# Gated attention and two feed-forward layers on one core: the state's product in quadrants, a first chunk without gap transfers, other fillers, and the last stores from two queues

## The chip, the cores and the metric

The kernel runs on one core of one Trainium2 chip. The metric is the device time of a run in microseconds; lower is better. The profile is of one execution, and its times count from the start of its span.

## The reference

For each of 4 batches and 8 heads a recurrence runs over 768 steps with a state of 48 x 48; its output is reordered to 3072 tokens of 384 features and goes through two feed-forward layers:

```python
for t in range(S):                     # q, k, v, alpha: (4, 8, 768, 48), float32
    state = alpha[:, :, t, :, None] * state + np.einsum('bhd,bhe->bhde', k[:, :, t], v[:, :, t])
    y[:, :, t] = np.einsum('bhd,bhde->bhe', q[:, :, t], state)
...
h = x @ w_in                           # 3072 x 384 by 384 x 2048
g = np.where(h > 0.0, h, np.exp(np.minimum(h, 0.0)) - 1.0)
x = g @ w_out                          # 2048 x 384
...
g = x @ w_gate                         # 384 x 1536
silu = g * (1.0 / (1.0 + np.exp(-g)))
out = silu * (x @ w_val) @ w_out       # 1536 x 384
```

## The kernel before

**Units.** The sequence is cut into 6 chunks of 128 steps. A chunk of one batch is a unit, 24 in all; a unit holds the 8 heads as 4 pairs, head j of a pair in partitions 64j to 64j+47 (`PR` = 112 partitions with the hole between them). A unit's input, 1 MB, has four parts: gate F, K, Q and V. VectorE scans F (`A`), VectorE, ScalarE and, from unit 4 on, GpSimd scale K and Q by the running product of the gates or its inverse (`N`, `M`). Then TensorE takes four steps: `Dk` transposes K (`flip`; ScalarE's `keep` copies it to KT), `E` makes the scores K'Q of each head (`scores`; VectorE's `causal` masks them into A), `Gs` makes the outer product of KT and V that renews the state (`outer`; VectorE's `state` adds and scales it into `sc[b]`), and `Hy` makes the output (`values`). For chunks after the first, `values` multiplies the state with Q by one 112 x 112 matmul a pair, with a block-diagonal copy `sbd` of the state that ScalarE makes in two instructions; it then adds V times A, one matmul for each head, 64 and 48 columns wide. All float32 matmuls show as two instructions each.

**Layout of x.** The result of a unit has 4 pairs of 2 x 48 rows, but the first layer wants 3 tiles of 128 rows. Pairs 0 to 2 go to rows 0 to 47 and 64 to 111 of the three tiles (`high`, and `low` or, in the first chunk, `minus` and `rest`, make the two float32r parts). The fourth pair goes to a tile `x3`, and when the four units of a chunk are there, `gaps` moves it by six DMAs in pieces of 16 rows into the holes. The rows of `w_in` are permuted to fit (`_feature_order`).

**Layers.** The first layer (`moe1`) makes, for each block f of 128 hidden features and 512 tokens, 9 matmuls of 512 columns into `h` and 9 into `acc`; between them ScalarE and VectorE compute elu and split it in two parts. It runs in the order of `SEGMENTS`: both of the first two chunks with the first half of the features, then both with the second half, then whole chunks. Units of a later chunk are mixed in. Weights come as int64 views of 768 KB (`weight`), and ScalarE and VectorE turn each into two float32r parts, three instructions each; two raw buffers (`RAWS`) take turns. The second layer (`moe2`) makes 18 matmuls into `gv` and 12 into `q` for each of 12 blocks in each of 6 chunks; for the last block of a chunk each of the four `q` tiles is copied out, in turn by ScalarE and VectorE, and stored by SP.

**Order.** Every step is put into a plan (`Plan.add`) with its engine, an assumed duration, and what it reads and writes. `Plan.run` schedules the list by assumed times and then issues it in the order of the planned starts, and `Pinned` keeps this order on each engine. `fill` is called before each planned TensorE step up to the first product of the first layer, with the planned gap in front of it; `warm` then issues bf16 matmuls on zeros (`idle` in the profile) for this gap, one for each 0.22 us:

```python
if ops[i][0] == "PE" and fill and start[i] <= start[until]:
    fill(start[i] - last)
    last = start[i] + ops[i][1]
...
for _ in range(int((us - 0.2) / 0.22)):
    ten.matmul(out=self.idle, lhsT=self.z, rhs=self.z[:, None, :].to_broadcast([128, 4, 128]), ...)
```

Before the plan, `at.warm(6.8)` (L821) issues such matmuls too. PSUM has two places that units share with nobody in the later chunks: `aps` (one bank: transpose, outer product, values) and `ape` (two banks: scores).

Of the kernel before, what the change touches and what calls it, by code (L numbers as in the profile page):

```python
# [18 lines left out]
DM = H * D  # L19
# [5 lines left out]
KD = DM // 128  # L25
TB = B * C
NF1, NF2 = F1 // 128, F2 // 128
G = 2
# [7 lines left out]
MINUS = B  # L36
# [5 lines left out]
class Plan:  # L42
# [25 lines left out]
    def run(self, fill=None, until=0):  # L68
# [72 lines left out]
def kernel(  # L141
# [52 lines left out]
    def weight(plan, pool, tag, src, slots):  # L194
# [5 lines left out]
        def load():  # L200
            w.raw = P.rp.tile([128, WT, 2], I32, tag="raw", name="raw")
            syn.dma_start(out=w.raw.rearrange("p a t -> p (a t)"), in_=src.bitcast(I32))
# [35 lines left out]
        plan.add("SP", 0.5, load, w=[hk, lk], kb=768)  # L238
# [22 lines left out]
    class Attention:  # L261
        def __init__(self, es):
# [7 lines left out]
            self.sbd = [cp.tile([128, NP, 128], F32, name=f"sbd{b}") for b in range(2)]  # L270
# [5 lines left out]
            self.neg = cp.tile([128, 128], F32R, name="neg")  # L276
            self.x3 = cp.tile([128, 2, TB], F32R, name="x3")
# [20 lines left out]
        def init(self):  # L298
            vec.memset(self.zero, 0.0)
# [4 lines left out]
            make_identity(nc, self.ident)  # L304
            vec.tensor_scalar(
# [8 lines left out]
            for t in self.sbd:  # L314
                nc.gpsimd.memset(t, 0.0)

        def warm(self, us):

            if self.idle is None:
                self.z = self.cp.tile([128, 128], BF16, name="wz")  # L320
                vec.memset(self.z, 0.0)
                self.idle = ph.tile([128, TB], F32, tag="h", name="idle")
            for _ in range(int((us - 0.2) / 0.22)):
# [94 lines left out]
        def Dk(self, u):  # L418
# [16 lines left out]
            plan.add("PE", 0.45, flip, r=[K], w=[key], soon=SOON, lag=MARGIN)  # L435
            plan.add("ACT", 0.48, keep, r=[key], w=["KT"])

        def E(self, u):
            d, (F, K, Q, V) = self.u[u], self.keys(u)
            c, b = divmod(u, B)  # L440
            if c:
                def state():
                    for j in range(2):
                        r = slice(64 * j, 64 * j + D)
                        act.activation(
                            out=self.sbd[u % 2][r, :, 64 * j:64 * j + D], in_=self.sc[b][r], func=AF.Copy)
                plan.add("ACT", 0.65, state, r=[("sc", b)], w=[("sbd", u % 2)])
# [25 lines left out]
            plan.add("PE", 1.25, scores, r=[K, Q], w=keys, soon=SOON, lag=MARGIN)  # L473
            plan.add("DVE", 1.24 if len(keys) > 1 else 1.1, causal, r=keys, w=["A"])

        def Gs(self, u):
# [27 lines left out]

            plan.add("PE", 0.75, outer, r=["KT", V], w=[key], soon=SOON, lag=MARGIN)
            plan.add("DVE", 0.65 if c else 0.3, state, r=[key, F], w=[("sc", b)])

        def Hy(self, u):
            d, (F, K, Q, V) = self.u[u], self.keys(u)
            c, b = divmod(u, B)  # L510
            key, bank = self.bank(u)
            ts = slice(b * C, (b + 1) * C)
            xk, gk = ("x", c % 2, b), ("x3", b)

            def values():
                v = d["v"]
                d["oy"] = o = bank()
# [7 lines left out]
                for p, cs in enumerate(cols):  # L525
                    ten.matmul(
                        out=o[0:64, cs], lhsT=v[:, 2 * p, :], rhs=d["A"][:, 0, p],
                        start=not c and p == 0, stop=p == NP - 1,
                    )
                    ten.matmul(  # L530
                        out=o[64:PR, cs], lhsT=v[:, 2 * p + 1, 0:D], rhs=d["A"][:, 1, p],
                        start=not c and p == 0, stop=p == NP - 1,
                    )
# [530 lines left out]
```

## Time and profile before

| what | value |
|---|---|
| median of 3 runs | 989.59 us (989.09 to 989.59) |
| the profiled execution's own time | 990.69 us |
| its span, first to last instruction | 988.9 us |
| TensorE busy | 98% of the span |
| VectorE, ScalarE, GpSimd busy | 55%, 52%, 7% |
| mean granted TensorE clock | 0.999 |
| share of `gv`, `q`, `h`, `acc` in the chain that ended last | 30%, 15%, 18%, 19% |

A busy time is the union of the instructions of an engine, fillers included; matmuls overlap, so that a busy TensorE can still be doing less than it could. The windows of the profile show the same by stage. In a timeline, instructions of one kind in a row are merged, with their count; what stands in brackets is how long the engine had been idle and what released it. PE is TensorE, DVE VectorE, ACT ScalarE, POOL GpSimd; SPq are the DMA issues of SP.

### The profile page before, as it was taken

Reading aid. Unit: us, or ns where it says so; the run is one execution under the profiler, and the core shown is the slowest. Engines: PE = TensorE matmul, PEld = TensorE weight load, DVE = VectorE, ACT = ScalarE, POOL = GpSimd, SP = SyncE. Lnnn points to the kernel's source line nnn. Section 1 sums busy time; section 2 is a strip of 40 time slices with the busy share of each in tenths; the row PEclk is TensorE's granted clock in tenths of the full one; section 3 lists DMA queues with packets and bytes.
Section 4 is the critical chain, followed back from the end, with each engine's and each line's share of the span. In section 5 each row is a group of like instructions: output and inputs, shape, how many; then the busy total and the mean of one; then the engine's idle time right before and its main releaser. Section 6 shows DMA issues by size and latency. Waiting matters only on the chain.

```text
span 988.9 us, 13352 instructions
## 1 busy us (share of the span) xinstructions
PE 973.4 (98%) x5354; PEld 811.2 (82%) x5354; DVE 541.0 (55%) x840; ACT 512.7 (52%) x910; POOL 69.3 (7%) x51
## 2 busy tenths in 40 slices
PE   9899999999999999999999999999999999999997
PEld 4577788878887888888888888888888888888886
DVE  4999888667646653533677763334333334333332
ACT  3889999666776765555898542212212212212111
POOL 0122011123211310100000000000000000000000
PEclk9999999999999999999999999999999999999999
DMA  4646434333302301100434311001001001000001
GB/s 192 222 158 209 162 114 159 108 102 118 101 1 85 129 6 43 36 14 1 160 128 183 127 52 65 1 1 64 1 1 57 8 1 45 9 1 32 1 1 36
DMA packets 20662, 72.51 MB, mean 73 GB/s; under 512 B 2672, under 2 KB 5744, under 8 KB 17648
## 3 DMA queue, kind: packets, MB, share of 16 engines
q1 hardware_dynamic: 20592, 71.58, 21.2%
q8 instruction: 44, 0.72, 0.3%
q14 instruction: 26, 0.21, 0.1%
HBM read 58.20 MB, written 11.01 MB: 70 GB/s over the span
## 4 chain that ended last, share of the span: by engine, by line
PE 91%; ACT 3%; DVE 3%; DMA 2%; issue 0%; SPq 0%; ACTq 0%; DVEq 0%
PE gv L128 30%; PE acc L128 19%; PE h L128 18%; PE q L128 15%; PE aps L128 4%; PE idle L128 2%; PE ape L128 2%; DMA in<-qkva 1%; DVE in L128 1%; ACT raw L128 1%; DVE raw L128 1%; DMA raw<-w 1%; ACT e L128 1%; ACT R L128 1%; ACT x L128 0%
## 5 line engine op out<-in xcount | busy, mean ns | idle before, releaser
L128 PE MATMUL gv<-x,wt 128*128 128x512 f32 x1296 | 308.1, 391 | 0.0
L128 PEld LDWEIGHTS gv<-x,wt 128*128 128x128 f32 x1296 | 242.2, 188 | 48.0
L128 PE MATMUL h<-x,wt 128*128 128x512 f32 x864 | 215.6, 394 | 1.4 <-DMA x<-x 1.4
L128 DVE TENSOR_TENSOR s<-gv,s 128x512 f32<-128x512 f32 x144 | 99.6, 691 | 210.7 <-ACT s L128 167.3
L128 PE MATMUL acc<-g,wt 128*128 128x512 f32 x864 | 214.5, 393 | 0.2 <-DVE g L128 0.2
L128 PEld LDWEIGHTS h<-x,wt 128*128 128x128 f32 x864 | 159.7, 188 | 37.0 <-ACT r L128 1.7
L128 PEld LDWEIGHTS acc<-g,wt 128*128 128x128 f32 x864 | 160.4, 188 | 35.0 <-DVE g L128 0.6
L128 PE MATMUL q<-wt,u 128*128 128x384 f32 x864 | 163.0, 337 | 0.0
L128 PEld LDWEIGHTS q<-wt,u 128*128 128x128 f32 x864 | 153.6, 188 | 5.6
L128 ACT ACTIVATE s<-gv 128x512 f32<-128x512 f32 x72 | 43.1, 598 | 176.6 <-PE gv L128 176.6
L128 DVE SCALAR_TENSOR_TENSOR e<-e,r 128x512 f32<-128x512 f32 x96 | 68.6, 715 | 98.0 <-ACT r L128 97.9
L128 ACT ACTIVATE u<-s 128x512 fp32r<-128x512 f32 x72 | 45.4, 631 | 123.6 <-DVE s L128 123.2
L128 ACT ACTIVATE e<-h 128x512 f32<-128x512 f32 x96 | 57.1, 595 | 67.8 <-PE h L128 67.4
L128 DVE TENSOR_TENSOR g<-e,g 128x512 fp32r<-128x512 f32 x96 | 67.3, 701 | 29.8 <-ACT g L128 29.5
L128 ACT ACTIVATE g<-e 128x512 fp32r<-128x512 f32 x96 | 60.3, 628 | 28.9 <-DVE e L128 28.5
L128 DVE SCALAR_TENSOR_TENSOR raw<-raw 128x768 int32<-128x768 int32 x68 | 67.9, 1000 | 12.0 <-ACT raw L128 10.9
L128 DVE TENSOR_TENSOR u<-s,u 128x512 fp32r<-128x512 f32 x72 | 49.8, 692 | 40.6 <-ACT u L128 40.5
L128 ACT ACTIVATE e<-e 128x512 f32<-128x512 f32 x96 | 60.7, 632 | 2.9
L128 ACT ACTIVATE raw<-raw 128x768 f32<-128x768 f32 x68 | 58.9, 905 | 3.1 <-DMA raw<-w 2.9
L128 ACT ACTIVATE r<-h 128x512 f32<-128x512 f32 x96 | 55.9, 582 | 0.0
L128 POOL TENSOR_TENSOR in<-in 112x512 f32<-112x512 f32 x20 | 30.1, 1504 | 249.9 <-DVE in L128 130.7
L128 POOL TENSOR_TENSOR in<-in,R 112x512 f32<-112x512 f32 x20 | 37.0, 1849 | 79.5 <-ACT R L128 79.5
(78 smaller groups left out, 614.7 us busy)
## 6 DMA issues: line engine op xcount, KB each, us to landing
raw<-w SPq DMA_DIRECT2D x34, 768.0 KB, 4.2
in<-qkva SPq DMA_DIRECT2D x23, 1024.0 KB, 5.4
x2r<-x2d SPq DMA_DIRECT2D x18, 256.0 KB, 3.4
out<-y SPq DMA_DIRECT2D x24, 192.0 KB, 2.0
x2d<-o SPq DMA_DIRECT2D x12, 256.0 KB, 2.3
x<-x SPq DMA_DIRECT2D x36, 64.0 KB, 4.3
half<-o SPq DMA_DIRECT2D x6, 256.0 KB, 4.0
part<-half SPq DMA_DIRECT2D x6, 256.0 KB, 6.1
```

Source lines behind the costliest of these rows:

```text
L128: ins = getattr(self.engine, name)(*a, **k)
```

## The change

Seven things change together.

1. **State's product.** `sbd` and its copies go. `values` multiplies `sc[b]` itself, 48 x 48 for each head, 8 matmuls instead of 4. Pairs 2 and 3 are written crosswise: head i of pair p goes to output half j = i xor `CROSS[p]`. V's product stands first, then the state's product in the order of pairs 0, 2, 1, 3, so that four matmuls in a row read and write the four quadrants. The output lies over the inner halves of the two banks of `ape`, no longer in `aps`.
2. **Joined steps.** From unit 4 on, scores and transpose of a unit are one step of the plan, and outer product and values another.
3. **First chunk.** `Hy` calls a new function `first`: it multiplies A of the fourth pair with V's 16-column pieces padded by zeros (`vz`, copied by GpSimd), so that the rows of the holes come out in their place. The first chunk has no `x3` and no `gaps`; one ScalarE instruction makes each part.
4. **Weights.** Because pairs are crossed, the third tile of `w_in` has its halves of 64 rows exchanged: each `w_in` load is three DMAs.
5. **Fillers.** `at.warm(6.8)` goes. The first gap gets one filler for each 0.36 us, later gaps one for each 0.25 us.
6. **Last chunk.** ScalarE issues the stores of tiles 0 and 2. The last tile is copied in halves by ScalarE and VectorE, and stored in halves by ScalarE and SP.
7. `gaps` of the later chunks reads the crossed rows.

```diff
@@ Plan.run @@
-                fill(start[i] - last)
+                fill(start[i] - last, last)
@@ weight @@
+            to, of, n = w.raw.rearrange("p a t -> p (a t)"), src.bitcast(I32), 2 * G * 128
+            if not cross:
+                syn.dma_start(out=to, in_=of)
+                return
+            m = n * CROSS.index(1)
+            syn.dma_start(out=to[:, 0:m], in_=of[:, 0:m])
+            for j in range(2):
+                syn.dma_start(
+                    out=to[64 * j:64 * j + 64, m:KD * n], in_=of[64 - 64 * j:128 - 64 * j, m:KD * n])
...
-        plan.add("SP", 0.5, load, w=[hk, lk], kb=768)
+        plan.add("SP", 1.5 if cross else 0.5, load, w=[hk, lk], kb=768)
@@ init, warm @@
+            self.z = self.cp.tile([128, 128], BF16, name="wz")
+            vec.memset(self.z, 0.0)
...
+            nc.gpsimd.memset(self.vz, 0.0)
...
-            for t in self.sbd:
-                nc.gpsimd.memset(t, 0.0)
...
-            for _ in range(int((us - 0.2) / 0.22)):
+            for _ in range(int((us - 0.2) / (0.25 if start else 0.36))):
@@ Dk, E @@
-            if c:
-                def state():
-                    for j in range(2):
-                        r = slice(64 * j, 64 * j + D)
-                        act.activation(
-                            out=self.sbd[u % 2][r, :, 64 * j:64 * j + D], in_=self.sc[b][r], func=AF.Copy)
-                plan.add("ACT", 0.65, state, r=[("sc", b)], w=[("sbd", u % 2)])
...
+                def both():
+                    scores()
+                    flip()
+                plan.add("PE", 1.65, both, r=[K, Q], w=[*keys, key], soon=SOON, lag=MARGIN)
+                plan.add("ACT", 0.48, keep, r=[key], w=["KT"])
@@ first @@
+            def apart():
+                pool.tensor_copy(
+                    self.vz[:, :, :, D:64],
+                    d["v"][:, 2 * KD:H, 0:D].rearrange("p j (i e) -> p j i e", i=KD))
+
+            def values():
+                d["oy"] = o = bank()
+                for p in range(KD):
+                    for j in range(2):
+                        i = j ^ CROSS[p]
+                        ten.matmul(
+                            out=o[64 * j:64 * j + 64, p * C:(p + 1) * C], lhsT=d["v"][:, 2 * p + i, :],
+                            rhs=d["A"][:, i, p], start=p == 0, stop=False)
+                for p in range(KD):
+                    for j in range(2):
+                        i = j ^ CROSS[p]
+                        ten.matmul(
+                            out=o[64 * j:64 * j + 64, p * C:(p + 1) * C], lhsT=self.vz[:, i, p],
+                            rhs=d["A"][:, i, KD], start=False, stop=p == KD - 1)
...
+            def high():
+                if 0 not in xt:
+                    new_x(0)
+                act.activation(
+                    out=xt[0][:, 0, :, ts], in_=d["oy"][:, 0:KD * C].rearrange("p (a c) -> p a c", a=KD),
+                    func=AF.Copy)
...
+            def minus():
+                ten.matmul(
+                    out=d["oy"][:, 0:KD * C], lhsT=self.neg, rhs=xt[0][:, 0, :, ts],
+                    start=False, stop=True, skip_group_check=True)
...
+            plan.add("POOL", 0.4, apart, r=[V], w=["vz"], port=True)
+            plan.add("PE", 1.5, values, r=["A", V, "vz"], w=[key], soon=SOON, lag=MARGIN)
+            plan.add("ACT", 0.45, high, r=[key], w=[xk])
+            plan.add("PE", 0.25, minus, r=[xk], w=[key], soon=SOON)
+            plan.add("ACT", 0.45, rest, r=[key], w=[xk])
@@ Hy, from unit 4 on @@
+                o = self.pe.tile([128, 2, 512], F32, tag="ape", name="ape").rearrange("p a n -> p (a n)")
+                d["oy"] = o = o[:, 256:768]
                 cols = [slice(p * C, (p + 1) * C) for p in range(NP)]
                 for p, cs in enumerate(cols):
-                    if c:
+                    for j in range(2):
+                        i = j ^ CROSS[p]
                         ten.matmul(
-                            out=o[0:PR, cs], lhsT=self.sbd[u % 2][0:PR, p, 0:PR], rhs=d["Q"][0:PR, p],
-                            start=p == 0, stop=False,
+                            out=o[64 * j:64 * j + (D if j else 64), cs],
+                            lhsT=v[:, 2 * p + i, 0:D] if j else v[:, 2 * p + i, :],
+                            rhs=d["A"][:, i, p], start=p % 2 == 0, stop=False,
                         )
...
+                for p in range(2):
+                    for pp in (p, p + 2):
+                        for i in range(2):
+                            j = i ^ CROSS[pp]
+                            r = slice(64 * i, 64 * i + D)
+                            ten.matmul(
+                                out=o[64 * j:64 * j + D, cols[pp]], lhsT=self.sc[b][r, pp],
+                                rhs=d["Q"][r, pp], start=False, stop=p == 1,
+                            )
...
+                def both():
+                    outer()
+                    values()
+                plan.add("PE", 2.2, both, r=["A", V, Q, "KT", ("sc", b)], w=[key, okey],
+                         soon=SOON, lag=MARGIN)
+                plan.add("DVE", 0.65, state, r=[okey, F], w=[("sc", b)])
@@ gaps, step @@
+                        k = 64 * (j ^ CROSS[i] ^ CROSS[KD]) + GAP * i
...
-            if b == B - 1:
+            if b == B - 1 and c:
                 self.gaps(c)
...
-            if nxt:
+            if nxt and u + 1 < B:
                 self.Dk(u + 1)
@@ moe2, last chunk @@
+                        def left(t=t, o=o, es=hs[0]):
+                            place()
+                            half(o.t[:, es], accs[t][:, es], 0)
+                            store(act, o, t, es)
...
+                        plan.add("ACT", 0.4, left, r=[("q", t)], w=[o.key])
+                        plan.add("DVE", 0.3, right, r=[("q", t)], w=["right"])
+                        plan.add("SP", 0.5, lambda t=t, o=o, es=hs[1]: store(syn, o, t, es), r=["right"])
...
+                        if end and t % 2 == 0:
+                            plan.add("ACT", 0.1, lambda t=t, o=o: store(act, o, t), r=[o.key])
@@ the start @@
-    at.warm(6.8)
     at.init()
```

## Rows read from the trace of the kernel before

**Rows 1.** page, part 1: busy us (share of the span) xinstructions
```profile
PE 973.4 (98%) x5354; PEld 811.2 (82%) x5354; DVE 541.0 (55%) x840; ACT 512.7 (52%) x910; POOL 69.3 (7%) x51
```

**Rows 2.** windows: length, busy us of each engine (instructions), clock, DMA share, GB/s
```profile
20.76:48.30 27.54, 23.57 (x245) 14.72 (x245) 26.98 (x49) 23.30 (x49) 2.59 (x2) 1.00 0.51 182
48.30:54.00 5.70, 4.82 (x49) 2.88 (x46) 4.55 (x10) 4.80 (x9) 1.86 (x1) 1.00 0.81 226
54.00:100.00 46.00, 44.73 (x332) 36.05 (x330) 45.57 (x70) 42.04 (x79) 12.30 (x8) 1.00 0.53 182
100.00:150.00 50.00, 49.67 (x269) 40.82 (x270) 42.62 (x59) 46.52 (x80) 4.64 (x3) 1.00 0.40 136
```

**Rows 3.** timeline, 0 to 30 us: start, length, engine, what [idle before]
```profile
1.07 18.50 PE L128 MATMUL idle<-wz 128*128 128x512 bf16 x72 [1.07 <-DVE zero L128]
...
9.85 0.69 DVE L128 SCALAR_TENSOR_TENSOR in<-N,in 112x512 f32<-112x512 f32 x1 [0.19 <-ACT N L128]
...
12.28 0.68 DVE L128 TENSOR_TENSOR in<-in 112x512 f32<-112x512 f32 x1
...
19.50 1.16 PE L128 MATMUL acc<-in 48*128 48x128 f32 x16
...
20.76 1.29 DVE L128 TENSOR_TENSOR A<-acc,mask 128x512 int32<-128x512 int32 x2 [7.80 <-PE acc L128]
```

**Rows 4.** timeline of TensorE, windows 2 to 6 and 8 to 12 us
```profile
1.47 4.90 PE L128 MATMUL idle<-wz 128*128 128x512 bf16 x11
...
7.75 4.48 PE L128 MATMUL idle<-wz 128*128 128x512 bf16 x20
```

**Rows 5.** timeline, 45 to 55 us
```profile
47.69 0.64 ACT L128 ACTIVATE x<-acc 112x128 fp32r<-112x128 f32 x2
...
48.36 3.94 SPq L128 DMA_DIRECT2D x<-x  x6
...
54.01 1.19 PE L128 MATMUL h<-x,wt 128*128 128x512 f32 x4
```

**Rows 6.** timeline of TensorE, one unit from 296 us
```profile
299.28 0.67 PE L128 MATMUL aps<-in,KT 128*64 128x48 f32 x16
299.88 2.33 PE L128 MATMUL h<-x,wt 128*128 128x512 f32 x9
302.05 1.04 PE L128 MATMUL aps<-in,sbd 112*112 112x128 f32 x8
303.02 1.09 PE L128 MATMUL aps<-A,in 128*64 128x128 f32 x16
304.03 2.35 PE L128 MATMUL acc<-g,wt 128*128 128x512 f32 x9
306.32 1.16 PE L128 MATMUL ape<-in 48*128 48x128 f32 x16
307.41 0.60 PE L128 MATMUL aps<-ident,in 112*128 112x112 f32 x4
307.78 2.29 PE L128 MATMUL h<-x,wt 128*128 128x512 f32 x9
```

**Rows 7.** timeline of TensorE, 30 to 60 us: a unit of the first chunk
```profile
36.09 0.67 PE L128 MATMUL acc<-in,KT 128*64 128x48 f32 x16
36.59 1.37 PE L128 MATMUL aps<-A,in 128*64 128x128 f32 x16
```

**Rows 8.** timeline of TensorE, 100 to 116 us: blocks with no unit between
```profile
102.52 2.20 PE L128 MATMUL acc<-g,wt 128*128 128x512 f32 x9
104.56 2.20 PE L128 MATMUL h<-x,wt 128*128 128x512 f32 x9
```

**Rows 9.** DMA issues at 2.5 to 2.8 us: count, KB each, us to landing
```profile
raw<-w SPq DMA_DIRECT2D x1, 768.0 KB, 12.0
```

**Rows 10.** timeline, 980 to 989 us
```profile
980.93 2.95 SPq L128 DMA_DIRECT2D out<-y  x4
...
981.98 0.56 DVE L128 COPY y<-q 128x384 f32<-128x384 f32 x1 [0.48 <-PE q L128]
```

More of the change, by code (lines that the diff above doesn't have):

```diff
@@ L25 @@
 KD = DM // 128
+CROSS = (0, 0, 1, 1)
 TB = B * C
@@ L191, in __init__, with weight @@
             self.key = key
-    def weight(plan, pool, tag, src, slots):
+    def weight(plan, pool, tag, src, slots, cross=False):
         w = Box(*turn(tag, slots))
@@ L433, in keep @@
                     out=d["KT"].rearrange("p a c -> p (a c)"), in_=d["ok"][:, 0:NP * PR], func=AF.Copy)
-            plan.add("PE", 0.45, flip, r=[K], w=[key], soon=SOON, lag=MARGIN)
-            plan.add("ACT", 0.48, keep, r=[key], w=["KT"])
+            if u < B:
+                plan.add("PE", 0.45, flip, r=[K], w=[key], soon=SOON, lag=MARGIN)
+                plan.add("ACT", 0.48, keep, r=[key], w=["KT"])
+            return key, flip, keep
         def E(self, u):
@@ L471, in causal @@
                     )
-            plan.add("PE", 1.25, scores, r=[K, Q], w=keys, soon=SOON, lag=MARGIN)
+            turned = self.Dk(u) if u >= B else None
+            if turned:
+                key, flip, keep = turned
+                def both():
+                    scores()
+                    flip()
+                plan.add("PE", 1.65, both, r=[K, Q], w=[*keys, key], soon=SOON, lag=MARGIN)
+                plan.add("ACT", 0.48, keep, r=[key], w=["KT"])
+            else:
+                plan.add("PE", 1.25, scores, r=[K, Q], w=keys, soon=SOON, lag=MARGIN)
             plan.add("DVE", 1.24 if len(keys) > 1 else 1.1, causal, r=keys, w=["A"])
@@ L503, in state, with first, rest @@
                 vec.tensor_tensor(out=sc[0:PR], in0=kv, in1=pc, op=ALU.mult)
+            if c:
+                return key, outer, state
             plan.add("PE", 0.75, outer, r=["KT", V], w=[key], soon=SOON, lag=MARGIN)
-            plan.add("DVE", 0.65 if c else 0.3, state, r=[key, F], w=[("sc", b)])
+            plan.add("DVE", 0.3, state, r=[key, F], w=[("sc", b)])
+        def first(self, u):
+            d, (F, K, Q, V) = self.u[u], self.keys(u)
+            key, bank = self.bank(u)
+            ts = slice(u * C, (u + 1) * C)
+            xk = ("x", 0, u)
+            def apart():
[26 more added lines that the diff above has]
+                    start=False, stop=True, skip_group_check=True)
+            def rest():
+                act.activation(
+                    out=xt[0][:, 1, :, ts], in_=d["oy"][:, 0:KD * C].rearrange("p (a c) -> p a c", a=KD),
+                    func=AF.Copy)
+            plan.add("POOL", 0.4, apart, r=[V], w=["vz"], port=True)
[3 more added lines that the diff above has]
+            plan.add("ACT", 0.45, rest, r=[key], w=[xk])
@@ L737, in load_split, with moe2 @@
         return b
-    def moe2(plan, x, xs, w2, pools, yp, put):
+    def moe2(plan, x, xs, w2, pools, yp, put, end=False):
         accs, us = {}, {}
@@ L804, in prep_w1 @@
         g, s = divmod(i, 2)
-        w1[g, s] = weight(plan, lambda: P.wp, "w", w1d[g, s], 2 * NG1)
+        w1[g, s] = weight(plan, lambda: P.wp, "w", w1d[g, s], 2 * NG1, not (plan.now or s))
     def prep_w2(plan, i, pool, n):
```

79 lines of the change are left out of this document (36 added, 43 removed).

## Prediction, on record before the result

> **What bounds the kernel now.** I read the page first, then the stages, then the timeline of the stage in which no engine ought to be waiting. The page says that TensorE is busy for 973.4 us of a 988.9 us span [rows 1], so time can come only from work that TensorE does and from TensorE work that is filler. The stages [rows 2] split the run. From 100 us on TensorE is full (49.67 of 50 us) and VectorE has slack (42.62). Between 20.76 and 100 us it is VectorE that is full: 26.98 of 27.54, then 4.55 of 5.70, then 45.57 of 46.00. All that it idles there is 0.56 + 1.15 + 0.43 = 2.1 us. The timeline of the first 25 us [rows 3] then shows what the page hides: 72 filler matmuls hold TensorE from 1.07 to 19.57 us. K of unit 0 is finished by VectorE at 9.85 + 0.69 = 10.54, VectorE runs out of other work at 12.28 + 0.68 = 12.96, and it then waits 7.80 us for the scores, which come behind the fillers at 19.50. So there are three regimes: a start bound by filler, a stretch to 100 us bound by VectorE, and the rest by TensorE.
>
> **Start.** The old call asks for int((6.8 - 0.2)/0.22) = 30 fillers before the plan; the other 42 of the 72 mean that the plan puts its first TensorE step at 42 to 43 times 0.22 plus 0.2, or 9.44 to 9.66 us. The 30 go, and the same gap divided by 0.36 gives 25 or 26. The fillers' spacing shows two levels [rows 4]: 11 in 4.90 us (0.45 each), later 20 in 4.48 us (0.22 each), that is, a clock of half and of full speed. The faster level was there by 7.75 us; from there to 19.57 about 53 fit, so some 19 were issued before. Of 26 fillers the last 7 take 7 x 0.22 = 1.5 us, and TensorE is free near 9.4 us, 1.1 us ahead of K. The scores (1.16 us) end before 12.96, so VectorE goes on without the wait: 20.76 - 12.96 = **7.8 us**. Nothing new is late there: the first weight piece lands 2.67 + 12.0 = 14.7 us after the start [rows 9], 1.7 us after VectorE goes on. From below, 6.5 us if that landing holds ScalarE up for most of this; from above, 19.50 - 10.54 = 9.0 us, TensorE's own wait.
>
> **First chunk without the transfer of gaps.** The first x is now whole when ScalarE has written it. Before, ScalarE ends at 47.69 + 0.64 = 48.33, six DMAs are issued for 3.94 us, and the first product starts at 54.01 [rows 5]. TensorE may thus start 5.7 us earlier relative to the others. But behind it VectorE is full to 100 us, and everything that it does there is due by then (elu, eight weight pieces, four units). TensorE would only wait in smaller portions. What can be won is VectorE's idle time of 2.1 us; I take half, **1.0 us** (0 to 5.7). The added cost lies on engines with cover: four more products of 128 columns a unit, in TensorE time that is filler anyway; one small GpSimd copy; and ScalarE writes one 384-column tile where it wrote two. If VectorE's queue were not the bound there, those products would cost about 4 x 4 x 0.12 = 2 us.
>
> **Weights in three transfers.** Eight loads become 24 issues on SP. At 3.94/6 = 0.66 us an issue [rows 5] each such load lands up to 1.3 us later, and unit loads queue behind it. Half of the eight fall into the VectorE stretch; two raw buffers cover most. I take **-0.5 us** (0 to -2.5).
>
> **A unit's TensorE work.** In the TensorE-bound part each microsecond of a unit counts, for 16 units (chunks 2 to 5); those of chunk 1 lie in VectorE's stretch. Step prices by start-to-start in one unit [rows 6]: the transposed K's outer product 0.60, the state's product 0.97 (8 instructions, 0.121 each), the product with V 1.01, scores 1.09 (16 instructions, 0.068 each: two of them run at once), transpose 0.37. A block of nine big matmuls takes 2.04 between others [rows 8], but 304.03 to 306.32 = 2.29 between two steps of split tiles, and 299.88 to 302.05 = 2.17 behind one. So entering or leaving a split costs 0.12 to 0.13.
> - Joining the outer product and V's product saves one leaving, 0.13. Where they already stand together the outer product takes 36.59 - 36.09 = 0.50, not 0.60 [rows 7]. Together 0.23.
> - The state's product: 8 instructions of 112 x 112 become 16 of 48 x 48. The trace has no four at a time. If four run at once, that is 4 steps of 0.121 = 0.48 instead of 0.97. If two, 8 steps: 0.97. If one, 16 steps: 1.94. The nearest rows are the scores (two row halves at once) and V's product (two column halves at once); nothing in them excludes both together, and the pairs are issued so that the two writers of one output half go to different banks. I take four, and 0.07 for the added change of form: saving 0.42.
> - In chunk 5 there is no outer product; V's product now needs an entry of 0.12 which the state's full-size product did not: saving 0.30.
> - Joining scores and transpose gives little, since they often stand together already (as at 307.41), and a small step that stands beside another today saves an entry and a leaving, 0.25, which the new order may lose. The new neighbours are unknown; I take off 0.1 a unit, 1.6 us.
>
> Sum: 12 x 0.65 + 4 x 0.30 - 1.6 = **7.4 us**; with two at once 16 x 0.49 = 7.8 us less, so -0.4; with one at once 16 x 1.46 = 23.4 us less, so -16. The ScalarE copies of the state (one of 0.7 us a unit) go too; from 100 us ScalarE is off the path, so this is worth nothing by itself.
>
> **End.** The last copy runs 981.98 to 982.54; the fourth store's issue ends at 980.93 + 2.95 = 983.88, 1.34 us behind it, because three issues stand ahead on SP [rows 10]. Halves shorten the copy by about 0.2 us (an estimate: less than half of 0.56, as a fixed part stays). An issue takes 2.95/4 = 0.74 us on average. SP's half then ends its issue near 981.98 + 0.36 + 0.74 = 983.1, 0.8 earlier; but ScalarE must issue the third tile's store before it copies its half, and issue again, which comes to 981.98 + 0.74 + 0.36 + 0.74 = 983.8, 0.1 earlier. I take half-way, **0.5 us** (-0.5 to 1.0).
>
> **Sum.** 7.8 + 1.0 - 0.5 + 7.4 + 0.5 = 16.2 us. The profiled execution took 990.69 us (span 988.9), so 974.5; the median of the runs is 1.1 lower, 989.59 - 16.2 = **973.4 us**.
>
> **Rivals.**
> - *The quadrants run two at a time.* The 16 small products need 8 steps, and the units' gain is gone: 973.4 + 7.8 = 981.2. For it: both halves of one pair write one PSUM bank, where the scores' halves today write different ones. Against it: V's two halves write one bank at once today, in disjoint output partitions. The Trainium skill (TensorEngine Tiling (Array Packing), Gotcha 1: PSUM Pressure) says that different row tiles cannot access the same PSUM bank simultaneously; taken literally for whole banks, it gives this rival's time. No row of this trace shows the case.
> - *The quadrants run one by one, and the kernel gets slower.* 16 steps a unit: 973.4 + 23.4 = 996.8, slower by 7.2. It decides from 16.2/16 = 1.0 us more for a unit's state product than I give it, that is above about 1.5 us. Against it: every split form in the trace overlaps at least in pairs.
> - *The early product counts in full.* If the plan can put off VectorE work beyond 100 us, where VectorE has 7.4 us of slack in 50, TensorE's 5.7 us come out whole: 973.4 - 4.7 = 968.7. Against it: all eight weight pieces were needed by then.
> - *The front gives back less.* Another wait takes the filler's place: the weight landing, SP's longer queue, or a TensorE clock at its lower level because fewer fillers bridge the gaps. Half of the start's 7.8 and nothing of the 1.0 would be left, 5 us less: 978.4. For it: the landing at 14.7 is close. Against it: VectorE waits for nothing else in 7.80 us.
>
> **How the numbers follow.** The forecast has 0.55, pairs 0.17, less at the front 0.13, the early product in full 0.10, one by one 0.05. The range runs from just below the third rival (967) to just above the first (982). A change of 0.2%, 2 us, is what a measurement of this kernel can tell from none. Only the one-by-one case is slower, 0.05; gains that add up to under 2 us, 0.01; the rest is faster, 0.94.
>
> **What would show it.** Filler: 25 or 26 of them ahead of the first scores, these near 10.6 us, and no VectorE wait of more than 1 us before the mask step. Start of the TensorE-bound part near 92 us, where it was 100.33. Small products in the 48 x 48 form, 16 in about 0.5 us; 0.97 or more means pairs. No DMA from x to x before the first big product, which starts near 40 us, with TensorE waits between 40 and 90 us of some 5 us in all. The last store's issue end about 1 us behind the last copy. The prediction falls if the quadrants don't overlap, or if VectorE is not the bound that I read between 20 and 100 us.

## The result, and the profile after

The changed kernel takes 981.7 us, median of 8 runs (977.56 to 984.53); the kernel before took 989.62 beside it (988.22 to 991.75). The ratio is 0.9917, with a 95% interval of 0.9898 to 0.9936. The gain is 7.9 us where 16.2 were forecast; the time lies inside the range, at its upper edge. The profiled execution took 980.24 us with a span of 978.8 us.

The page's busy times and its granted clock in 40 slices:

```profile
PE 955.5 (98%) x5471; PEld 797.8 (82%) x5471; DVE 544.7 (56%) x840; ACT 498.6 (51%) x863; POOL 74.1 (8%) x54
PEclk8989999999999999999999999999999999999999
```

TensorE's busy time, fillers included, fell by 17.9 us and the span only by 10.1 [rows 1], so waits came in, and the clock line says where to look: slices 1 and 3, the first 75 us. The same stages as in [rows 2], cut where the changed kernel has them: first mask, first big product, first big product of chunk 1, and 50 us more (length, then busy us of PE, PEld, DVE, ACT and POOL, granted clock, DMA share, GB/s):

```profile
14.45:43.21 28.76, 23.80 (x253) 16.31 (x251) 26.39 (x45) 20.63 (x35) 4.51 (x6) 0.86 0.44 149
43.21:99.22 56.01, 48.44 (x400) 37.71 (x400) 51.19 (x82) 44.42 (x80) 18.30 (x9) 0.94 0.59 187
99.22:149.22 50.00, 50.00 (x271) 41.03 (x272) 42.69 (x58) 46.49 (x79) 7.00 (x4) 1.00 0.45 152
```

VectorE, which idled 2.1 us between 20.76 and 100 us before, now idles 28.76 + 56.01 - 26.39 - 51.19 = 7.2 us ahead of chunk 1. The clock is below full in both stages, where it was full before. Two stretches hold most of that, and a third comes ahead of them, around the first scores:

```profile
11.70:19.00 7.30, 7.30 (x58) 5.12 (x60) 7.04 (x15) 5.72 (x10) 0.00 (x0) 0.53 0.50 159
...
39.00:43.00 4.00, 3.44 (x42) 2.85 (x38) 4.00 (x8) 2.11 (x4) 1.22 (x2) 0.57 0.00 0
...
56.00:63.90 7.90, 7.34 (x47) 5.82 (x49) 6.96 (x9) 6.24 (x11) 0.78 (x1) 0.57 0.37 133
```

The start of TensorE's timeline, beside [rows 3]:

```profile
1.07 8.53 PE L128 MATMUL idle<-wz 128*128 128x512 bf16 x29 [1.07 <-DVE zero L128]
11.69 0.57 PE L128 MATMUL aps<-ident,in 112*128 112x112 f32 x4 [2.08 <-DVE in L128]
12.24 2.08 PE L128 MATMUL acc<-in 48*128 48x128 f32 x16
```

The fillers end at 9.60, and then TensorE idles for 2.08 us, because VectorE finishes K of unit 0 at 10.89 + 0.69 = 11.58 where it was 10.54 before. A scan of the next unit now stands ahead of it:

```profile
7.57 1.37 DVE L128 TENSOR_TENSOR_SCAN in<-in,zero 112x128 f32<-112x128 f32 x4 [0.65 <-DMA in<-qkva]
...
10.89 0.69 DVE L128 SCALAR_TENSOR_TENSOR in<-N,in 112x512 f32<-112x512 f32 x1
```

When TensorE goes on, its clock falls to the lower level (0.50, 1.2 of 2.4 GHz), and the scores take 2.08 us where they took 1.16. The first mask still starts at 14.45 instead of 20.76.

TensorE's waits over the whole span (us in total, times, longest):

```profile
PE h L128 <- DMA x<-x: 3.4, 1, 3.4
PE acc L128 <- ACT KT L128: 3.3, 2, 2.6
PE ape L128 <- DVE x L128: 2.7, 1, 2.7
PE aps L128 <- DVE in L128: 2.1, 1, 2.1
```

The third is new in kind: a unit's output now lies in `ape`, so the next unit's scores wait until VectorE has copied that output out. It ends at 56.56, just where the lower clock of the third stretch begins. The first is the transfer of gaps for chunk 1; SP's issues (first fence) and TensorE (second) show it:

```profile
85.16 2.36 SPq L128 DMA_DIRECT2D raw<-w  x4
87.75 0.40 SPq L128 DMA_DIRECT2D in<-qkva  x1
88.41 5.55 SPq L128 DMA_DIRECT2D x<-x  x6
```

```profile
93.61 2.20 PE L128 MATMUL acc<-g,wt 128*128 128x512 f32 x9
99.22 2.08 PE L128 MATMUL h<-x,wt 128*128 128x512 f32 x8 [3.41 <-DMA x<-x]
```

One unit in the TensorE-bound part, beside [rows 6]:

```profile
286.03 1.16 PE L128 MATMUL ape<-in 48*128 48x128 f32 x16
287.12 0.60 PE L128 MATMUL aps<-ident,in 112*128 112x112 f32 x4
287.50 2.30 PE L128 MATMUL h<-x,wt 128*128 128x512 f32 x9
289.72 0.61 PE L128 MATMUL aps<-in,KT 128*64 128x48 f32 x15
...
290.23 1.05 PE L128 MATMUL ape<-A,in 128*64 128x128 f32 x15
291.21 0.65 PE L128 MATMUL ape<-in,sc 48*48 48x128 f32 x16
291.79 1.19 PE L128 MATMUL acc<-g,wt 128*128 128x512 f32 x4
```

The state's product runs from 291.21 to the next start at 291.79, 0.58 us, where it took 0.97. The end, beside [rows 10]:

```profile
970.75 1.54 SPq L128 DMA_DIRECT2D out<-y  x2
971.20 0.34 ACTq L128 DMA_DIRECT2D out<-y  x1
971.21 0.36 DVE L128 COPY y<-q 128x192 f32<-128x192 f32 x1 [0.49 <-PE q L128]
971.67 0.33 ACT L128 ACTIVATE y<-q 128x192 f32<-128x192 f32 x1 [0.49 <-DVE y L128]
972.03 0.34 ACTq L128 DMA_DIRECT2D out<-y  x1
```

The two halves are not copied side by side: ScalarE's waits for VectorE's to end.

So the profile splits the gain at the first big product of chunk 1: it starts 100.33 - 99.22 = 1.1 us earlier than before, and from there to the first product of the second layer it is 433.22 - 423.55 = 9.7 us shorter. The units seem to have paid, and the front not. The experiments take that apart.

### The profile page after: what moved, and what is told of

The parts are those of the page before. It is cut to its first block, busy times and chain, and to the rows that moved or that the text cites. A ratio compares the mean times of both kernels' runs of the same rounds, so it can differ in the third digit from the quotient of the medians.

```text
span 978.8 us, 13568 instructions
## 1 busy us (share of the span) xinstructions
PE 955.5 (98%) x5471; PEld 797.8 (82%) x5471; DVE 544.7 (56%) x840; ACT 498.6 (51%) x863; POOL 74.1 (8%) x54
## 4 chain that ended last, share of the span: by engine, by line
PE 91%; DVE 4%; DMA 2%; issue 1%; ACT 1%; SPq 0%; ACTq 0%; DVEq 0%
PE gv L128 30%; PE acc L128 20%; PE h L128 19%; PE q L128 15%; PE ape L128 5%; PE aps L128 2%; DMA in<-qkva 1%; DVE in L128 1%; DMA x<-x 1%; DVE raw L128 1%; DVE A L128 0%; DVE wt L128 0%; SPq L128 0%; DVE e L128 0%; DVE x L128 0%
## 5 line engine op out<-in xcount | busy, mean ns | idle before, releaser
L128 ACT ACTIVATE raw<-raw 128x768 f32<-128x768 f32 (+1 forms) x68 | 59.2, 908 | 3.4 <-DMA raw<-w 3.0
L128 POOL TENSOR_TENSOR in<-in 112x512 f32<-112x512 f32 x20 | 36.3, 1813 | 206.4 <-DVE in L128 124.1
L128 ACT ACTIVATE R<-R 112x512 f32<-112x512 f32 x48 | 30.2, 630 | 20.6 <-DVE R L128 20.0
```

The source lines that it names most:

```text
L128: ins = getattr(self.engine, name)(*a, **k)
```

## The experiments

Theory A: the fillers and the units gave what the prediction said, and the first chunk's new form, the three transfers of `w_in` and the clock that falls behind new waits took half of it back ahead of chunk 1. Theory B: the fillers themselves gave less, or the four quadrants don't run at once. The runs came in three batches, each timed beside runs of the kernel before on the same chip: b1, e1, e2 and e3 (its median there 989.06 us), then e4, e5, e7 and e9 (989.69), then f1, f2, e10 and e6 (989.35). The ratio is to these runs. It takes in all runs of a kernel, so that it can say something else than the medians, which take the middle one.

| kernel | median us (range), runs | ratio, 95% interval | first mask | first big product | of chunk 1 | second layer | span's end |
|---|---|---|---|---|---|---|---|
| before (profile) | 989.62 (988.22-991.75), 8 | | 20.76 | 54.01 | 100.33 | 533.55 | 988.9 |
| changed | 981.7 (977.56-984.53), 8 | 0.9917, 0.9898-0.9936 | 14.45 | 43.21 | 99.22 | 522.77 | 978.8 |
| b1_nofill | 981.9 (980.95-983.29), 5 | 0.9926, 0.9913-0.9939 | 12.59 | 45.47 | 93.04 | 524.83 | 980.2 |
| e1_fill | 980.18 (978.12-981.85), 5 | 0.9906, 0.9892-0.9920 | 14.55 | 42.98 | 97.44 | 522.62 | 978.7 |
| e2_keep | 979.11 (977.75-980.9), 4 | 0.9904, 0.9889-0.9918 | 14.40 | 42.32 | 96.70 | 520.31 | 976.3 |
| e3_gapq | 981.26 (978.73-984.51), 6 | 0.9924, 0.9907-0.9941 | 14.49 | 42.93 | 97.32 | 522.79 | 978.1 |
| e4_oneload | 977.06 (974.68-977.45), 4 | 0.9866, 0.9845-0.9887 | 14.37 | 41.87 | 94.93 | 519.89 | 975.0 |
| e5_pairs | 979.19 (976.74-982.87), 6 | 0.9893, 0.9872-0.9915 | 14.84 | 43.08 | 97.76 | 521.54 | 977.6 |
| e7_split | 978.22 (978.01-980.6), 5 | 0.9888, 0.9870-0.9906 | 15.31 | 47.31 | 95.31 | 523.58 | 978.6 |
| e9_nofirst | 977.63 (976.12-982.94), 6 | 0.9894, 0.9868-0.9920 | 12.41 | 51.57 | 97.00 | 520.54 | 975.1 |
| f1_mix | 974.4 (972.96-975.68), 5 | 0.9848, 0.9833-0.9863 | 12.58 | 46.32 | 92.90 | 516.51 | 971.1 |
| f2_combo | 974.87 (974.54-977.07), 5 | 0.9854, 0.9838-0.9869 | 12.12 | 49.18 | 95.14 | 520.28 | 974.9 |
| e10_nocross | 986.01 (983.09-987.06), 6 | 0.9954, 0.9938-0.9971 | 14.44 | 40.78 | 96.38 | 527.24 | 984.1 |
| e6_tail | 979.95 (979.52-980.28), 4 | 0.9902, 0.9887-0.9918 | 14.38 | 42.27 | 98.26 | 521.96 | 977.6 |

The last five columns are of the profiled execution, in us: four starts, and the end of the span. Up to chunk 1 every kernel has done the same 14 blocks of nine matmuls of the first layer, so the starts can be compared.

**b1_nofill: the kernel before with the new fillers alone.**

```diff
-            for _ in range(int((us - 0.2) / 0.22)):
+            for _ in range(int((us - 0.2) / (0.25 if start else 0.36))):
...
-    at.warm(6.8)
```

> The kernel before with the change of the fillers alone: no 30 fillers ahead of the plan, one for each 0.36 us of the first gap and each 0.25 us of later ones. The prediction's term for the start says that VectorE's wait of 7.8 us goes and the whole kernel follows: 982 us. If the clock falls when fillers do not reach to the first scores, some of it is given back: 984 to 986. If the front was not bound by VectorE, 987 or more.

Measured: 7.2 us faster than before, where the prediction's term was 7.8. The start of its timeline:

```profile
1.07 7.75 PE L128 MATMUL idle<-wz 128*128 128x512 bf16 x25 [1.07 <-DVE zero L128]
10.31 1.16 PE L128 MATMUL acc<-in 48*128 48x128 f32 x16 [1.49 <-DVE in L128]
11.41 0.60 PE L128 MATMUL aps<-ident,in 112*128 112x112 f32 x4
```

There are 25 fillers (forecast 25 or 26). The scores stand ahead of the transpose, start at 10.31 (forecast 10.6 for the change) and take 1.16. The clock is at 1.00 over the whole front, and VectorE idles 1.9 us from the first mask to chunk 1, as little as before. So the fillers are not what the change lost by, and fewer fillers did not bring the lower clock by themselves.

**e1_fill and e2_keep: more fillers in the changed kernel.** e1 asks for one filler per 0.31 us of the first gap; e2 adds to this 11 bf16 matmuls ahead of the output of unit 3, in the second idle stretch.

```diff
-            for _ in range(int((us - 0.2) / (0.25 if start else 0.36))):
+            for _ in range(int((us - 0.2) / (0.25 if start else 0.31))):
...
+                if u == B - 1:
+                    self.keep_up(self.idle, 11)
                 d["oy"] = o = bank()
```

> The changed kernel with one filler for each 0.31 us of the first gap instead of 0.36, some 33 or 34 fillers where there were 29, so that TensorE's idle time of 2.08 us ahead of its first step shrinks to about 1.1 us. If the fall of TensorE's clock behind that gap (0.79, then 0.50 from 11 to 19 us) costs the front its gain, the clock stays at 1.00 there, the first scores take 1.1 us instead of 2.08, and the kernel is 1 to 3 us faster, as little as 1 if other falls follow. If VectorE alone sets the front, the clock changes and the time stays within 0.5 us.

> The same, and 11 more fillers ahead of the values of unit 3, where TensorE idles for 2.56 us at 36 us and its clock falls again (0.57 from 39 to 43 us). By the theory of the clock another 0.5 to 1.5 us faster than with the first fillers alone; by the theory that VectorE sets the front nothing, within 0.5 us. The third fall at 54 to 62 us, behind a wait of 2.75 us for VectorE, is left as it is.

Measured: 1.5 and 2.6 us under the changed kernel, chunk 1 at 97.44 and 96.70 instead of 99.22. Around the first scores the clock is 1.00 in both profiles and the scores take 1.16 us, as expected, but it falls elsewhere (0.67 from 36 to 46 us in e1, 0.76 from 50 to 60 us in e2). The gain points to a clock that costs something, but e5 and e6, near copies of the change without more fillers, came out at 979.19 and 979.95, so most of it is scatter. The clock's own price is not settled by these two.

**e3_gapq: chunk 1's gap transfers issued by ScalarE's queue.**

```diff
-                        syn.dma_start(
+                        (act if c == 1 else syn).dma_start(
```

> The changed kernel with the six gap transfers of chunk 1 issued from ScalarE's queue instead of SP's; all other orders are the same. By the theory that the front's gain is lost behind the loads that SP issues just ahead of these transfers (about 2.5 MB at 85 to 88 us, landing 8.7 us behind the fourth issue, TensorE waits 3.41 us), they land within 5 us, the wait of 3.41 us ends, the first product of chunk 1 starts near 96 us instead of 99.22, and the kernel is about 3 us faster. If the 16 DMA engines are just full, the queue does not matter and the time stays within 1 us; ScalarE's issues of some 3 us could cost up to 1 us.

Measured: the wait for the transfer is gone, chunk 1 starts 1.9 us earlier, and nothing is gained at the end (981.26): from there to the second layer it takes 425.47 us, 1.9 more than in the changed kernel. The transfers did not land within 5 us either; they took 7.7 us from ScalarE's queue, 8.8 from SP's. And the edit made a wait of its own: ScalarE's six issues take 4.46 us, and VectorE waits 4.07 us for the `R` that ScalarE makes behind them. TensorE's largest wait in the profile is then for VectorE's elu, 2.67 us from 92.0:

```profile
85.83 4.46 ACTq L128 DMA_DIRECT2D x<-x  x6
...
91.00 0.69 DVE L128 SCALAR_TENSOR_TENSOR N<-in,R 112x512 f32<-112x512 f32 x1 [4.07 <-ACT R L128]
```

```profile
PE acc L128 <- DVE g L128: 3.9, 3, 2.7
```

So e3 replaced one wait by another, and what the transfer's wait cost by itself is not shown by it.

**e4_oneload: `w_in` in one transfer each.** The halves of the third tile are exchanged in the array's layout ahead of the kernel. The load's assumed cost in the plan goes back from 1.5 to 0.5 with it, so the planned order changes too.

```diff
-        w1[g, s] = weight(plan, lambda: P.wp, "w", w1d[g, s], 2 * NG1, not (plan.now or s))
+        w1[g, s] = weight(plan, lambda: P.wp, "w", w1d[g, s], 2 * NG1, plan.now and not s)
...
+    r[KD - 1] = r[KD - 1, ::-1].copy()
```

> The changed kernel with the crossed halves of the third tile of w_in already exchanged in the layout of the array, so that each w_in load is one DMA of 768 KB again, with its old assumed cost in the plan. The prediction's term for the three transfers says 0.5 us faster, at most 2.5. If the queue of SP is what takes the front's gain, ScalarE's waits for raw weights and the landing of the gap transfers shrink and it is 2 to 4 us faster. If VectorE's new waits are the cause, within 1 us.

Measured: 977.06, which is 2.1 under e5 of the same batch (2.7 by the ratios, whose intervals overlap) and 4.6 under the changed kernel, whose own runs of before were alike (989.62 and 989.69). DMA issues between 14 and 100 us (count, KB each, median us from issue to landing) of the changed kernel and then of e4:

```profile
raw<-w SPq DMA_DIRECT2D x4, 768.0 KB, 5.1
raw<-w SPq DMA_DIRECT2D x4, 512.0 KB, 6.3
raw<-w SPq DMA_DIRECT2D x8, 128.0 KB, 6.4
x<-x SPq DMA_DIRECT2D x6, 64.0 KB, 8.8
```

```profile
raw<-w SPq DMA_DIRECT2D x8, 768.0 KB, 4.8
x<-x SPq DMA_DIRECT2D x6, 64.0 KB, 5.0
```

Split weights land 1.5 to 1.6 us later than whole ones (0.5 to 0.6 in e5) and the gap transfers 3.8 us later. Chunk 1 starts without a wait for x, 4.3 us earlier. The later gap transfers are not the work of the split alone: with one load each they took 7.9 us in f2 and 7.4 in e10. What is smaller with whole loads, in both pairs of kernels that differ in them, are ScalarE's waits for raw weights between 14 and 100 us (total, times, longest; e5 and e4, then e9 and f2, which come below):

```profile
ACT raw L128 <- DMA raw<-w: 1.9, 2, 1.0
ACT raw L128 <- DMA raw<-w: 0.5, 2, 0.3
ACT raw L128 <- DMA raw<-w: 6.6, 4, 3.0
ACT raw L128 <- DMA raw<-w: 2.8, 3, 1.9
```

VectorE idles as long ahead of chunk 1 as in the changed kernel (7.3 and 7.2 us) but has done less work by then, from the first mask on (73.25 us instead of 77.58). No run separates the transfers from the planned order that their assumed cost changes. The clock did not set the earlier start: e4 has the lower level in the same places (0.66 from 10 to 20 us in both; 0.83, 0.81 and 0.85 in the three stretches of 10 us from 40, where the changed kernel has 0.86, 0.83 and 0.83).

**e5_pairs: the state's product in the order of pairs 0, 1, 2, 3**, so that consecutive pairs share quadrants.

```diff
-                for p in range(2):
-                    for pp in (p, p + 2):
+                for p in (0, 2):
+                    for pp in (p, p + 1):
```

> The changed kernel with the state's product in the order of pairs 0, 1, 2, 3 instead of 0, 2, 1, 3, so that matmuls in a row use two quadrants and not four. If four quadrants do run at once, the 16 small products take about 0.97 us a unit instead of about 0.6, and the 16 units from chunk 2 on cost 6 to 7 us more. If only two overlapped anyway, nothing changes.

Measured: the 16 products take 0.67 us instead of 0.65, with the next step 0.59 behind their start, where it was 0.58; the kernel 979.19.

```profile
289.87 0.67 PE L128 MATMUL ape<-in,sc 48*48 48x128 f32 x16
```

The order of issue is worth nothing here, and e5 serves as a copy of the change for its batch.

**e10_nocross: e4 with nothing crossed**, so that the state's product lies in two quadrants, not four.

```diff
-CROSS = (0, 0, 1, 1)
+CROSS = (0, 0, 0, 0)
```

> The one-load kernel with nothing crossed, so that the state's product lies in two quadrants instead of four; all else stays. If four quadrants run at once in the change: the 16 small products take about 1.1 us instead of 0.65, 16 units x 0.45 = 7 us more than the one-load kernel, near 984. If they run two at a time in the change as well: no difference, near 977.

Measured: 986.01, a ratio of 0.9954 against e4's 0.9866, or 8.7 us more, with intervals far apart. One unit:

```profile
292.25 1.08 PE L128 MATMUL ape<-in,sc 48*48 48x128 f32 x16
293.26 0.73 PE L128 MATMUL acc<-g,wt 128*128 128x512 f32 x2
```

The state's product now takes 1.01 us to the next start, 0.43 more, or 6.9 us in 16 units. The stretch from chunk 1 to the second layer is 430.86 - 424.96 = 5.9 us longer; the rest came ahead of chunk 1 (1.45) and behind the last matmul (1.8). So four do run at once in the change, and only the crossing makes them.

**e7_split: chunk 1's units in single steps** (scores, transpose, outer product and values each planned by itself).

```diff
-            if u < B:
+            if u < 2 * B:
                 plan.add("PE", 0.45, flip, r=[K], w=[key], soon=SOON, lag=MARGIN)
```

> The changed kernel with the steps of chunk 1 (units 4 to 7) planned singly, as before: scores, transpose, outer product and values. The values still share the scores' banks. By the theory that joined steps make VectorE wait in the front (7.0 us idle from the first mask step to the first product of chunk 1, where the kernel with other fillers alone has 1.6), that product starts 2 to 4 us earlier than 99.2 and the kernel gains as much. If the shared banks or the falls of the clock cause the waits, within 1 us.

Measured: 978.22, 1.0 under e5 with intervals that overlap almost wholly. Inconclusive: chunk 1 starts earlier (95.31), but from there to the second layer it takes 428.27 us where e5 takes 423.78. Two outer products of chunk 1's units (at 107.28 and 120.79) and a stretch at the lower clock (0.83 from 90 to 100 us) now stand behind that start or around it. The profiled span ends no earlier.

**e9_nofirst: the first chunk's output as before** (four pairs, `x3`, gap transfers, with the crossed rows).

```diff
-            if u < B:
-                self.first(u)
-                return
...
-            if b == B - 1 and c:
+            if b == B - 1:
                 self.gaps(c)
```

> The changed kernel with the first chunk's output as before: fourth pair into its own tile, subtraction in two matmuls, six gap transfers; pairs crossed. The prediction's term says that the form without gap transfers saves 1.0 us (0 to 5.7), so this is 1 us slower. If the new form's extra matmuls, GpSimd copies and its changed order in the plan cost the front its gain, it is 1 to 4 us faster.

Measured: 977.63, 1.6 under e5 by the medians, but level by the ratios (0.9894 and 0.9893): four of the six runs lie between 976.12 and 978.34, two at 982.53 and 982.94. Neither side of the expectation is shown. The first big product comes 8.5 us later than in e5 and the kernel is no slower: the earlier product that the first chunk's new form bought brings nothing that shows at the end. The first mask is at 12.41 in place of 14.84; among the kernels with the new fillers it lies at 14.37 to 15.31 in all with the new form, and at 12.12 to 12.59 in all without it.

**f1_mix: fillers, units from chunk 2 on and end of the change; both first chunks as before; `w_in` in one transfer.** It takes the edits of e4 and e9, and keeps `sbd` and single steps for chunk 1:

```diff
-            if u < B:
+            if u < 2 * B:
                 plan.add("PE", 0.45, flip, r=[K], w=[key], soon=SOON, lag=MARGIN)
...
+            if c == 1:
+                def copies():
...
-            if c:
+            if c > 1:
```

> The fillers, joined units, quadrants and end of the change, with the first two chunks as before (the first chunk's output with its gap transfers left as before, chunk 1 with its block copies, planned step by step) and each w_in half in one load; in that one array the halves are exchanged ahead. Theory A (the front lost to VectorE waits and to TensorE's clock what the units won): the fillers-only kernel's 981.9 less the units' 7.4, so 974.5 (973 to 976.5); first big product of chunk 1 near 93 us, no stretch before 100 us with a granted clock under 0.95 once the fillers are over. Theory B (the joined units themselves carry the loss, by less than 7.4 us in their own part): 978 to 980, although chunk 1 starts near 93.

Measured: 974.4, Theory A's 974.5. The stages as for the changed kernel:

```profile
12.58:46.32 33.74, 26.62 (x276) 17.16 (x275) 32.80 (x57) 29.76 (x64) 6.19 (x4) 0.96 0.57 193
46.32:92.90 46.58, 44.68 (x331) 35.97 (x331) 45.78 (x75) 41.15 (x80) 8.76 (x7) 1.00 0.57 189
92.90:142.90 50.00, 50.00 (x271) 40.87 (x272) 41.88 (x62) 47.07 (x79) 5.59 (x4) 1.00 0.47 157
```

VectorE idles 0.94 + 0.80 = 1.7 us ahead of chunk 1, and chunk 1 starts at 92.90, as in b1. From there to the second layer it takes 423.61 us, like the changed kernel's 423.55 and 8.2 less than b1's 431.79. So the gain that the changed kernel lacks lies in the three edits that f1 undoes together, the first chunk, chunk 1's new form and the three transfers; f1 does not say how it divides. One thing was not as expected: a short stretch at the lower clock (below, in the last section).

**f2_combo: e4 and e9 together**, chunk 1 as in the change.

> The change with the first chunk's output as before and w_in's halves in one load each, that is, both edits that gave 1.6 and 2.1 us each against the pairs kernel. If the two losses are separate: near 975.5, first big product of chunk 1 at 93 to 95 us. If both are the same lost time of VectorE before chunk 1: near 977, first product of chunk 1 near 95 to 97. The clock falls before 60 us should be there still, since chunk 1's shared bank stays.

Measured: 974.87. Against e9 (977.63) the one transfer gives 2.8 by the medians and 4.0 by the ratios, whose intervals just touch. Against e4 (977.06) the old first chunk gives 2.2 and 1.2, which is not resolved. The time is the one expected of separate losses, but the start of chunk 1 (95.14) lies between the two expectations; that the losses add is not shown. Both edits undone together give 3.9 us against e5 and 6.2 against the changed kernel, by the ratios; that is clear of the scatter. Against f1 the new form of chunk 1 costs 0.5, which is not resolved. Yet the profiled execution (976.76, the second slowest of the five) had VectorE idle for 6.5 us ahead of chunk 1 and a clock of 0.78 between 40 and 54 us, so idle time there is not all lost time.

**e6_tail: the change without its new end.**

```diff
-            lambda t, c=c: rows[c, t], c == NCH - 1)
+            lambda t, c=c: rows[c, t])
```

> The change without its edit of the end: the last tile copied whole by one engine and all last stores issued from SP, as before. By the prediction's term 0.5 us longer than the change in the stretch behind the last matmul. By the rival reading (ScalarE's half waits for VectorE's half, and its queue closes later) 0.6 us shorter: last matmul to end of the span 6.9 us instead of 7.6. The time of the whole within 1 us of the change either way, so the profile decides; beside the other three it is also the run nearest to the change itself.

Measured: 7.27 us from the end of the last matmul to the span's end, against 7.61 in the changed kernel; but with the new end the other ten kernels showed from 6.22 to 8.50 (median of all eleven 6.94), and with the old one before, b1 and e6 showed 6.96, 6.96 and 7.27. Neither expectation can be told from this scatter, and the time (979.95) tells nothing either. In the four runs the granted clock was 0.992 each time, and the times lie within 0.8 us.

## Why the prediction came out at half the gain

**What bounds the kernel: right for the kernel before.** VectorE is the bound ahead of chunk 1 and TensorE behind it. b1 and f1 leave VectorE 1.9 and 1.7 us of idle time there and both reach chunk 1 at 93 us (forecast 92). The changed kernel does not keep VectorE full there: it idles 7.2 us, and chunk 1 starts at 99.22.

**Start, 7.8 forecast: 7.2 measured in b1.** The mechanism was right, and so were the 25 fillers and, within 0.3 us, the start of the scores at 10.31. In the change itself there were 29 fillers and the scores came at 12.24, because the first chunk's new form moved VectorE's and TensorE's order: with the old form, in e9, they come at 10.13 behind 25 fillers.

**Units, 7.4 forecast: right.** f1's gain over before (14.95) less b1's (7.16) is 7.8 us for the units and the end together, some 2 us either way by the ratios' intervals, forecast 7.4 + 0.5. The state's product took 0.58 where 0.55 was assumed; the smaller gains of the joined steps were not measured apart. The first rival, pairs, is refuted by e10: two at a time cost 0.43 us a unit. The Trainium skill's rule beside it (TensorEngine Tiling (Array Packing), Gotcha 1: PSUM Pressure: different row tiles cannot access one PSUM bank at the same time) does not hold in this case for tiles that write disjoint partitions of a bank: in the change each bank gets products of both row halves, and 16 of them start and end within 0.65 us, where the two-quadrant form takes 1.08. The second rival, one by one, falls with it.

**First chunk without gaps, +1.0 forecast: not seen.** Undoing it gives nothing (e5 to e9) and 1.2 us (e4 to f2) by the ratios, 1.6 and 2.2 by the medians, with intervals that overlap; neither a small gain nor a loss is resolved. The term counted the added work as covered, but the reach of the new form was wider: it changed the order ahead of the first mask (14.84 in e5 and 12.41 in e9, 14.37 in e4 and 12.12 in f2). The first big product came 8.5 us earlier and nothing of it reached the end, which refutes the third rival, the early product in full: by it e9 would be 5.7 us slower.

**Weights in three transfers, -0.5 forecast: about -3.3.** This is the step that failed. By the ratios the loss is 2.7 us (e5 to e4) and 4.0 (e9 to f2), on average 3.3 with some 2.1 either way (an estimate from the four intervals); by the medians 2.1 and 2.8. The later landing was forecast at up to 1.3 us, and it was 0.3 to 1.6. What was wrong is that "two raw buffers cover most": ScalarE waited 1.9 us for raw weights in e5 and 6.6 in e9, and 0.5 and 2.8 with whole loads. That these waits carry the loss is argued, since the planned order changed with them. The two terms together were forecast at +0.5 and came out at -3.9 (f2 against e5) to -6.2 (f2 against the changed kernel).

**End, 0.5 forecast: not resolved.** The last issue does end earlier, 1.20 us behind the last matmul in place of 1.94 (1.19 to 2.02 in the eleven kernels with the new end). But that ScalarE's half waits for VectorE's half was not seen, and what follows the issue scatters by more than the term.

**The rival that came true in part: the front gives back less.** It was priced at 5 us with a chance of 0.13. Of its three causes the weights had a part. For SP's longer queue it is not shown: chunk 1's gap transfers landed in 8.8 us instead of 2.4 before, but nearly as late from ScalarE's queue (7.7 in e3) and with whole loads (7.9 in f2). They were quick, 2.4 to 3.9 us, in the kernels that had issued their last weights some 8 us or more ahead of them (before, b1, f1). The third cause, a lower clock, is there in the changed kernel's profile, but not because of fewer fillers: b1 has the same rule for them and a clock of 1.00. The waits that the other edits made came ahead of it, among them the wait for the shared `ape` that the prediction overlooked when it moved the output there.

What f1 shows for the start, the units and the end is 15.0 us. Less 3.3 for the weights, and the unresolved 0.6 for the first chunk and 0.5 for chunk 1's new form (f1 to f2), that is 10.6 us, or 979.0, near the copies e5 (979.19) and e6 (979.95). That they meet proves little, since the terms come from differences to e5 and its neighbours. The changed kernel's own median is some 2 us above these copies. Its eight runs go with their granted clock, from 977.56 at 0.993 to 984.53 at 0.987, and at 0.992 it took 979.74, as e6 did. What sets the clock of a run was not settled.

The time of 981.7 lies in the range by luck. It stands beside the 981.2 of the first rival, whose cause e10 refutes; the losses that led there lie ahead of chunk 1, and the rival that had put them there stood at 978.4.

## What to carry to other kernels

A stage that is bound by one engine gains nothing from another engine's earlier start: the first big product came 8.5 us later in e9 and the kernel was no slower. When a load is cut in pieces, ask which engine will wait for it and how long, and not only how much later it lands. When a wait is moved, look for the one that the move makes: in e3 the issues on ScalarE held up VectorE. Split small products over all four quadrants of TensorE where they fit. And undo edits afterwards, one by one and together, since here two of the seven took back part of what the others gave: without them the kernel takes 974.87 us (f2), and 974.4 with chunk 1 undone as well (f1).

## What the runs showed of the hardware that was not expected

The length of an idle stretch of TensorE did not by itself decide whether its clock fell. In e10 TensorE does next to nothing from 8.9 to 11.7 us (columns as above) and the clock stays at 1.00:

```profile
8.90:11.70 2.80, 0.02 (x1) 0.06 (x1) 2.70 (x6) 1.54 (x3) 0.78 (x1) 1.00 1.00 419
11.70:19.00 7.30, 6.59 (x71) 4.10 (x71) 7.26 (x16) 6.39 (x11) 0.75 (x1) 1.00 0.47 170
```

In f1 it idled 1.66 us from 8.6, worked on, and then had the lower clock for most of 12 to 16 us:

```profile
12.00:16.00 4.00, 4.00 (x37) 2.59 (x36) 4.00 (x10) 3.87 (x7) 0.00 (x0) 0.57 0.53 221
```

b1, with 1.49 us at the same place, kept 1.00; e3 kept it too, from 10 to 20 us, although TensorE had waited 2.9 us for VectorE ahead of its first step.

Small products in different quadrants ran at once whatever the order in which their pairs were issued (0.65 and 0.67 us for 16), so the four quadrants did not need neighbours in the stream to be of different quadrants.
